# First batch of an attention and mixer kernel: down-sampled sums moved between engines, a smaller mask build, two tiles on other PSUM banks

## The chip, the core and the metric

One core of a Trainium2 chip runs the whole kernel. The metric is the device time of one execution in microseconds. Of the kernel before, three runs took 659.92, 660.85 and 661.27 us; the median is 660.85 us.

## What is computed

The reference, cut to what matters (B = 4 batches, H = 8 heads, S = 576 positions, D = 64 per head, DM = 512):

```python
q_d, k_d, v_d = (t.reshape(B, H, S // 4, 4, D).mean(axis=3) for t in (q, k, v))
low   = repeat(softmax(q_d @ k_d.T / 8) @ v_d, 4, axis=2)
local = softmax(where(abs(i - j) < 4, q @ k.T / 8, -1e9)) @ v
x = (low + local), heads side by side            # B x S x 512
gate = sigmoid(causal 5-tap convolution of x)
x = (gate * (x @ w_val)) @ w_out
h = relu(x.T @ w_tok1) @ w_tok2                  # mixes positions
u = x + h.T
out = u + relu(u @ w_ch1) @ w_ch2
```

## The kernel before

**Stages.** For each batch, `attention(b)` makes x and the gate, `p1(b)` makes u (products with w_val, w_out, w_tok1, w_tok2), and `c1(b)` the first channel product, whose result goes to DRAM. `c2()` does the second channel product for all batches at the end. Large products run three times, as high times high, high times low and low times high parts (`mm3`, lines 217 to 219). The weights arrive as 64-bit words and are decoded on VectorE (lines 135 to 143).

**Order.** Batches 1 to 3 of the attention are mixed into the main stream of products by a table of times, and from `p1(0)` on the order of TensorE is the program's own. Batch 0 comes before all of it, with nothing to hide behind, and its order on each engine is set by a scheduler. `busy(n)` (lines 105 to 108) puts products of zeros between its steps, 80 in all ("fillers", tile `idle_ps`).

**Attention of batch 0.** The four pairs of heads (hp 0 to 3) each go through the same steps:

- `sums` (line 285): q and k of four neighbouring positions are added. In batch 0 this is four matmuls with the identity into PSUM (line 294) and a copy by ScalarE (line 295); in the other batches one `tensor_reduce` of VectorE (line 297). The four parts of v are added in two steps on GpSimd (lines 300 and 301).
- `low_scores` (304) makes the low-resolution scores `sc_d` (line 311), `loc_scores` (347) the local ones `sc_l` in two tiles of 6 and 4 windows: one bf16 matmul writes the mask (line 353), 64x64 matmuls add the scores (line 359).
- `softmax` (251): maximum on VectorE (258), exponentials one window at a time on ScalarE (264), division by the sum on VectorE in batch 0 and on GpSimd in the others (269; the engine is chosen in line 276).
- `low_turn` and `loc_turn` transpose the weights (lines 324, 373), and ScalarE copies them out (327, 377). `low_out` multiplies by the summed v (line 339, tile `o_d`), `loc_out` by v (line 388, tile `o_l`). VectorE adds the two (394), and `conv` follows (401, 404).

After hp 3, `hi_lo` (494 on ScalarE, 495 on GpSimd) splits x, and the first product `p_val` of `p1(0)` can run.

**PSUM.** Eight banks in four tags of two: `as`, `ao`, `m`, `n`. In batch 0, `sc_l` takes both banks of `m`, so the local scores of a pair wait until the exponentials of the pair before have read theirs. `o_d` and `o_l` take `n`, all else but `sc_d` takes `ao`, the fillers too.

**Mask and identity.** GpSimd builds the mask for all ten windows at once (lines 89 to 98); VectorE casts the identity to bf16 (line 88).

**Transfers.** All are issued by SP in a fixed order. A w tile has three buffers, so its load waits for VectorE to have decoded an earlier one.

Of the kernel before, what the change touches and what calls it, by code (L numbers as in the profile page):

```python
# [14 lines left out]
AF = mybir.ActivationFunctionType  # L15
ALU = mybir.AluOpType
AX = mybir.AxisListType
# [3 lines left out]
B, H, S, D = 4, 8, 576, 64  # L21
NHP = H // 2
CQ = 58
WIN = 64
NCK = 10
PADW = CQ * (NCK - 1) + WIN + 3
SD = S // 4
# [30 lines left out]
TAG0 = {"sc_d": "as", "sc_l": "m", "o_d": "n", "o_l": "n"}  # L58
# [12 lines left out]
NEG = -8.0e9  # L71
# [3 lines left out]
def kernel(ctx, tc, qk, vw, v4, w_val, conv_w, w_out, w_tok1, w_tok2, w_ch1, w_ch2, out):  # L75
    nc = tc.nc
# [5 lines left out]
    def T(p, shape, dt, tag, bufs, name=None):  # L82
        return p.tile(shape, dt, tag=tag, bufs=bufs, name=name or tag)

    ident = T(sb, [128, 128], F32, "ident", 1)
    make_identity(nc, ident)
    ident16 = T(sb, [128, 128], BF16, "ident16", 1)
    nc.vector.tensor_copy(out=ident16, in_=ident)
    mask = T(sb, [128, NCK, WIN], BF16, "mask", 1)
    nc.gpsimd.memset(mask, 0.0)  # L90
    for h in range(2):
        m = mask[64 * h:64 * h + 64]
        nc.gpsimd.affine_select(out=m, in_=m, compare_op=ALU.is_ge, fill=NEG, base=0,
                                pattern=[[0, NCK], [1, WIN]], channel_multiplier=-1)
        nc.gpsimd.affine_select(out=m, in_=m, compare_op=ALU.is_ge, fill=NEG, base=6,
                                pattern=[[0, NCK], [-1, WIN]], channel_multiplier=1)
        nc.gpsimd.memset(m[:, 0, 0:3], NEG)
        nc.gpsimd.memset(m[:, NCK - 1, S - (CQ * (NCK - 1) - 3):WIN], NEG)
    cw = T(sb, [128, KC, TAPS], F32, "cw", 1)


# [66 lines left out]
    def w_sq(key, src):  # L168
        return load_w(key, [[r] for r in rows_of(src, 0, DM)], "w2", NW)
# [81 lines left out]
    def softmax(parts, e, scale, mult):  # L251

        P, n, w = e.shape
        mx = T(sb, [P, n], F32, f"mx{P}", NM, name="mx")
        sm = T(sb, [P, n], F32, f"sm{P}", NM, name="sm")
        o = 0
        for p in parts:
            nc.vector.tensor_reduce(out=mx[:, o:o + p.shape[1]], in_=p, axis=AX.X, op=ALU.max)
            o += p.shape[1]
        nc.scalar.activation(out=mx, in_=mx, func=AF.Copy, scale=-scale)  # L260
        o = 0
        for p in parts:
            for c in range(p.shape[1]):
                nc.scalar.activation(out=e[:, o, :], in_=p[:, c, :], func=AF.Exp, scale=scale,  # L264
                                     bias=mx[:, o:o + 1], accum_out=sm[:, o:o + 1])
                o += 1
        nc.scalar.activation(out=sm, in_=sm, func=AF.Copy, bias=1e-9)
        nc.vector.reciprocal(out=sm, in_=sm)
        mult.tensor_tensor(out=e, in0=e, in1=bc(sm, w), op=ALU.mult)

    def attention(b):
# [3 lines left out]
        early = lambda: tc.high_priority(offset=PRI) if b else nullcontext()  # L275
        mult = nc.gpsimd if b else nc.vector

        def bank(shape, name):
            if b:
                tag = "as" if name[:2] == "sc" else "ao"  # L280
            else:
                tag = TAG0.get(name, "ao")
            return T(ps, shape, F32, tag, BANKS[tag], name=name)

        def sums(hp):
            d = hpd[hp]
            w = d.pop("v4")
            qk_d = T(sb, [128, 2, SD], F32, "qkd", ND, name="qk_d")
            qd, kd = qk_d[:, 0], qk_d[:, 1]
            qk_4 = d["qk"][:, :, 3:3 + S].rearrange("p i (a r) -> p i a r", r=4)  # L290
            if b == 0:
                p = bank([128, 2, SD], "qk_d")
                for r in range(4):
                    nc.tensor.matmul(p, lhsT=ident, rhs=qk_4[:, :, :, r], start=(r == 0), stop=(r == 3))  # L294
                nc.scalar.activation(out=qk_d, in_=p, func=AF.Copy)
            else:
                nc.vector.tensor_reduce(out=qk_d, in_=qk_4, axis=AX.X, op=ALU.add)
            d["qkd"] = qd, kd
            vd = T(sb, [72, 2, 128], F32, "vd", NVD, name="vd")
            nc.gpsimd.tensor_tensor(out=w[:, 0:2], in0=w[:, 0:2], in1=w[:, 2:4], op=ALU.add)  # L300
            nc.gpsimd.tensor_tensor(out=vd, in0=w[:, 0], in1=w[:, 1], op=ALU.add)
            d["vd"] = [vd]

        def low_scores(hp):
            d = hpd[hp]
            qd, kd = d.pop("qkd")
            parts = [bank([72, 2, SD], "sc_d") for _ in range(2)]
            for c in range(2):
                for h, p in enumerate(parts):
                    r0 = 64 * h  # L310
                    nc.tensor.matmul(p[:, c, :], lhsT=qd[r0:r0 + 64, c * HD:c * HD + HD],
                                     rhs=kd[r0:r0 + 64, :], start=True, stop=True)
            e = d["ed"] = T(sb, [72, 4, SD], F32, "e", NE, name="e_d")
            softmax(parts, e, 0.125 / 16.0, mult)

        def low_turn(hp):
            d = hpd[hp]
            e = d.pop("ed")
            ts = d["pd"] = []
            for h in range(2):  # L320
                p = bank([72, 2, 2, HD], "pt_d")
                for kc in range(2):
                    for c in range(2):
                        nc.tensor.transpose(p[:, kc, c, :], e[:, 2 * h + c, kc * HD:kc * HD + HD], ident[0:72, 0:72])
                t = T(sb, [72, 2, 2, HD], F32, "pt", NPT, name="pts_d")
                with early():
                    nc.scalar.activation(out=t, in_=p, func=AF.Copy)
                ts.append(t)
# [17 lines left out]
        def loc_scores(hp):  # L346
            d = hpd[hp]
            qk = d["qk"]
            parts = []
            for c0, c1 in LU:  # L350
                n = c1 - c0
                p = bank([128, n, WIN], "sc_l")
                nc.tensor.matmul(p.rearrange("p a w -> p (a w)"), lhsT=ident16,
                                 rhs=mask[:, c0:c1, :].rearrange("p a w -> p (a w)"), start=True, stop=False)
                for c in range(n):
                    o = CQ * (c0 + c)
                    for h in range(2):
                        r0 = 64 * h
                        nc.tensor.matmul(p[r0:r0 + 64, c, :], lhsT=qk[r0:r0 + 64, 0, 3 + o:3 + o + WIN],  # L359
                                         rhs=qk[r0:r0 + 64, 1, o:o + WIN], start=False, stop=(c == n - 1))  # L360
                parts.append(p)
            e = d["el"] = T(sb, [128, NCK, WIN], F32, "e", NE, name="e_l")
            softmax(parts, e, 0.125, mult)
# [50 lines left out]
        if b:  # L414

            hpd[0] = load(b, 0)
            hpd[0]["v"] = load_v(b, 0)
            yield
            sums(0)
            for i in range(NHP + 1):  # L420
                if i < NHP:
                    low_scores(i)
                    yield
                if i:
                    low_turn(i - 1)
                    yield
                if i < NHP:
                    loc_scores(i)
                    yield
                if i + 1 < NHP:  # L430
                    hpd[i + 1] = load(b, i + 1)
                    sums(i + 1)
                if i:
                    low_out(i - 1)
                    yield
                    loc_turn(i - 1)
                    yield
                    loc_out(i - 1)
                    conv(i - 1)
                    yield  # L440
                if i + 1 < NHP:
                    hpd[i + 1]["v"] = load_v(b, i + 1)
# [15 lines left out]
        def scores(hp):  # L458
            loc_scores(hp)
            yield  # L460
            sums(hp)
            low_scores(hp)
            yield
# [258 lines left out]
    w = chain(w_sq("val", w_val), w_sq("out", w_out))  # L722
# [56 lines left out]
```

## Time and profile before

| | |
|---|---|
| median of three runs | 660.85 us (659.92 to 661.27) |
| the profiled execution's own time | 661.05 us |
| its span, first to last instruction | 659.1 us |
| busy: TensorE, its weight loads, VectorE, ScalarE, GpSimd | 622.6, 531.7, 341.6, 300.6, 165.3 us |
| mean granted clock of TensorE | 0.976 of full |
| first `p_val` product / the one from which they run on without a gap | 75.25 us / 81.76 us |

The profiled execution lies 0.2 us over the median, and 1.95 us of its time lie outside the span. In the rows below times count from the start of the span. PE is TensorE, DVE VectorE, ACT ScalarE, POOL GpSimd, and SP issues the transfers. The profile prints some names without their digits: `v_sb` stands for both the tile of four v parts (`v4_sb`, loaded in line 236) and the v windows (loaded in line 245), `ident_68` is the bf16 identity, `w` the 64-bit weight tile. One fp32 matmul call shows as two records.

### The profile page before, as it was taken

How to read it: one execution, taken by the hardware profiler on the slowest of the kernel's cores; microseconds unless marked ns; L12 is line 12 of the kernel's file. 1: busy time of each engine (PE TensorE's matmuls, PEld its weight loads, DVE VectorE, ACT ScalarE, POOL GpSimd, SP SyncE). 2: the span in 40 equal slices, each digit the busy share in tenths (PEclk: the TensorE clock that was granted, in tenths of full speed). 3: DMA queues.
4: the chain of work that ended last, by engine and by line, in shares of the span. 5: the costliest groups of instructions: out<-in, count | busy, mean ns of one | idle time of the engine just before them, and what ended most of it. 6: DMA issues, size and time to landing. Idle time of an engine off the chain costs nothing.

```text
span 659.1 us, 12794 instructions
## 1 busy us (share of the span) xinstructions
PE 622.6 (94%) x4920; PEld 531.7 (81%) x4920; DVE 341.6 (52%) x689; ACT 300.6 (46%) x1032; POOL 165.3 (25%) x183
## 2 busy tenths in 40 slices
PE   6999697988889999999999999999999999999997
PEld 3454496777888988998998999998898888888887
DVE  4478987897886476533344434106637242424232
ACT  1666537555657564547645635324433222222221
POOL 4213521325325413514331413204523000000000
PEclk8999988988889999999999999999999999999999
DMA  8841322456783255783322486565997354553220
GB/s 246 220 150 52 105 61 75 155 184 199 256 287 133 81 192 152 251 250 116 106 71 74 148 252 205 166 191 189 294 311 280 96 161 159 155 164 124 85 79 33
DMA packets 53901, 107.23 MB, mean 163 GB/s; under 512 B 5776, under 2 KB 21392, under 8 KB 53840
## 3 DMA queue, kind: packets, MB, share of 16 engines
q1 hardware_dynamic: 53840, 106.42, 51.5%
q8 instruction: 38, 0.62, 0.4%
q14 instruction: 23, 0.19, 0.1%
HBM read 76.52 MB, written 29.88 MB: 161 GB/s over the span
## 4 chain that ended last, share of the span: by engine, by line
PE 69%; DVE 10%; DMA 8%; ACT 5%; POOL 3%; issue 3%; SPq 0%; DVEq 0%; POOLq 0%; ACTq 0%
PE p_o L217 8%; PE p_o L219 7%; PE p_o L218 7%; PE g_ps L217 5%; DMA w<-in_w_ch_dram 5%; PE g_ps L218 5%; PE g_ps L219 4%; PE sc_l L359 3%; DMA v_sb<-in_v_dram 2%; PE p_val L218 2%; PE qk_d L294 2%; PE p_val L217 2%; PE p_val L219 2%; ACT e_l L264 2%; PE p_x L217 2%
## 5 line engine op out<-in xcount | busy, mean ns | idle before, releaser
L217 PE MATMUL g_ps<-u_hl,w_hl 128*128 128x288 f32 x384 | 117.0, 305 | 0.7 <-DVE u_sb L612 0.7
L218 PE MATMUL g_ps<-u_hl,w_hl 128*128 128x288 f32 x384 | 114.1, 297 | 1.2 <-POOL u_hl L495 1.1
L219 PE MATMUL g_ps<-u_hl,w_hl 128*128 128x288 f32 x384 | 113.5, 296 | 0.0
L217 PE MATMUL p_o<-g_hl,ch 128*128 128x512 f32 (+1 forms) x240 | 88.7, 370 | 0.9 <-ACT r_sb L641 0.9
L219 PE MATMUL p_o<-g_hl,ch 128*128 128x512 f32 (+1 forms) x240 | 88.5, 369 | 0.0
L218 PE MATMUL p_o<-g_hl,ch 128*128 128x512 f32 (+1 forms) x240 | 88.5, 369 | 0.0
L495 DVE TENSOR_TENSOR g_hl<-r_back,g_hl 128x512 fp32r<-128x512 f32 (+1 forms) x60 | 38.4, 641 | 92.9 <-ACT g_hl L494 87.4
L494 ACT ACTIVATE g_hl<-r_back 128x512 fp32r<-128x512 f32 (+1 forms) x60 | 35.2, 588 | 107.5 <-PE p_o L219 105.2
L217 PEld LDWEIGHTS g_ps<-u_hl,w_hl 128*128 128x128 f32 x384 | 72.4, 189 | 4.0 <-issue 2.7
L218 PEld LDWEIGHTS g_ps<-u_hl,w_hl 128*128 128x128 f32 x384 | 72.6, 189 | 2.1 <-POOL u_hl L495 2.1
L219 PEld LDWEIGHTS g_ps<-u_hl,w_hl 128*128 128x128 f32 x384 | 72.6, 189 | 0.0
L641 ACT ACTIVATE r_sb<-g_ps 128x288 f32<-128x288 f32 x96 | 39.0, 408 | 57.8 <-PE g_ps L219 50.3
L404 DVE SCALAR_TENSOR_TENSOR gate_sb<-x_f,cw,gate_sb 128x575 f32<-128x575 f32 (+5 forms) x68 | 60.7, 900 | 0.8
L217 PEld LDWEIGHTS p_o<-g_hl,ch 128*128 128x128 f32 x240 | 45.2, 188 | 9.3 <-ACT r_sb L641 1.7
L219 PEld LDWEIGHTS p_o<-g_hl,ch 128*128 128x128 f32 x240 | 45.2, 189 | 7.7
L218 PEld LDWEIGHTS p_o<-g_hl,ch 128*128 128x128 f32 x240 | 45.3, 189 | 7.6
L264 ACT ACTIVATE e_l<-sc_l,mx 128x64 f32<-128x64 f32 x160 | 48.2, 332 | 0.8
L495 POOL TENSOR_TENSOR x_hl<-x_f,x_hl 128x288 fp32r<-128x288 f32 x32 | 32.5, 1028 | 59.9 <-ACT x_hl L494 59.9
L217 PE MATMUL p_val<-x_hl,val_hi 128*128 128x288 f32 x128 | 41.1, 321 | 5.2 <-ACT x_hl L494 3.1
L218 PE MATMUL p_val<-x_hl,val_hi 128*128 128x288 f32 x128 | 40.0, 313 | 1.5 <-POOL x_hl L495 1.5
L135 DVE TENSOR_SCALAR wa<-w 128x256 int32<-128x256 int32 (+2 forms) x76 | 25.1, 343 | 30.8 <-DMA w<-in_w_ch_dram 16.9
L217 PE MATMUL p_x<-y_hl,out_hi 128*128 128x288 f32 x128 | 39.8, 311 | 1.4 <-ACT u_sb L546 0.7
(110 smaller groups left out, 1324.2 us busy)
## 6 DMA issues: line engine op xcount, KB each, us to landing
w_hl<-w_dr SPq DMA_DIRECT2D x36, 512.0 KB, 4.4
r_dr<-r_sb SPq DMA_DIRECT2D x48, 288.0 KB, 4.3
w<-in_w_ch_dram SPq DMA_DIRECT2D x48, 256.0 KB, 3.2
r_back<-r_dr SPq DMA_DIRECT2D x48, 256.0 KB, 2.8
qk_sb<-in_qk_dram SPq DMA_DIRECT2D x16, 589.0 KB, 4.0
w_dr<-w_hl SPq DMA_DIRECT2D x12, 512.0 KB, 2.9
v_sb<-in_vw_dram SPq DMA_DIRECT2D x16, 320.0 KB, 13.7
v_sb<-in_v_dram SPq DMA_DIRECT2D x16, 288.0 KB
```

The costliest lines, as they stand in the source:

```text
L135: nc.vector.tensor_scalar(a, high, 3, 0x3FFFFFF8, ALU.logical_shift_left, ALU.bitwise_and)
L217: nc.tensor.matmul(out_ap, lhsT=lh, rhs=rh, start=first, stop=False)
L218: nc.tensor.matmul(out_ap, lhsT=lh, rhs=rl, start=False, stop=False)
L219: nc.tensor.matmul(out_ap, lhsT=ll, rhs=rh, start=False, stop=last)
L264: nc.scalar.activation(out=e[:, o, :], in_=p[:, c, :], func=AF.Exp, scale=scale, bias=mx[:, o:o + 1], accum_out=sm[:, o:o + 1])
L294: nc.tensor.matmul(p, lhsT=ident, rhs=qk_4[:, :, :, r], start=(r == 0), stop=(r == 3))
L359: nc.tensor.matmul(p[r0:r0 + 64, c, :], lhsT=qk[r0:r0 + 64, 0, 3 + o:3 + o + WIN], rhs=qk[r0:r0 + 64, 1, o:o + WIN], start=False, stop=(c ...
L404: nc.vector.scalar_tensor_tensor(out=g[:, t0:s1], in0=x[:, t0 - sh:s1 - sh], scalar=cw[:, hp, k:k + 1], in1=g[:, t0:s1], op0=ALU.mult, op1 ...
L494: nc.scalar.activation(out=hi_ap, in_=src_ap, func=AF.Copy)
L495: lo_eng.tensor_tensor(out=lo_ap, in0=src_ap, in1=hi_ap.bitcast(F32), op=ALU.subtract)
L641: paced[0] = nc.scalar.activation(out=r[:, hv(hs)], in_=p[:, 0:HS], func=AF.Relu)
```

## The change

The bf16 identity is built by GpSimd. The mask's pattern is built for one window and copied to the others, all on GpSimd. In batch 0 the sums of q and k are made by VectorE's `tensor_reduce`, as in the other batches; the four identity matmuls and ScalarE's copy go. The v parts of batch 0 are not added beforehand: `low_out` runs over all four, so `o_d` accumulates 16 matmul calls for a pair of heads and not 4. The local scores of hp 1 take the banks `n`. The line that chooses the engine of the softmax division is the same in both kernels.

```diff
@@ -85,17 +85,20 @@
     ident = T(sb, [128, 128], F32, "ident", 1)
     make_identity(nc, ident)
     ident16 = T(sb, [128, 128], BF16, "ident16", 1)
-    nc.vector.tensor_copy(out=ident16, in_=ident)
+    make_identity(nc, ident16)
     mask = T(sb, [128, NCK, WIN], BF16, "mask", 1)
-    nc.gpsimd.memset(mask, 0.0)
+    one = mask[:, 1, :]
+    nc.gpsimd.memset(one, 0.0)
     for h in range(2):
-        m = mask[64 * h:64 * h + 64]
+        m = one[64 * h:64 * h + 64]
         nc.gpsimd.affine_select(out=m, in_=m, compare_op=ALU.is_ge, fill=NEG, base=0,
-                                pattern=[[0, NCK], [1, WIN]], channel_multiplier=-1)
+                                pattern=[[1, WIN]], channel_multiplier=-1)
         nc.gpsimd.affine_select(out=m, in_=m, compare_op=ALU.is_ge, fill=NEG, base=6,
-                                pattern=[[0, NCK], [-1, WIN]], channel_multiplier=1)
-        nc.gpsimd.memset(m[:, 0, 0:3], NEG)
-        nc.gpsimd.memset(m[:, NCK - 1, S - (CQ * (NCK - 1) - 3):WIN], NEG)
+                                pattern=[[-1, WIN]], channel_multiplier=1)
+    nc.gpsimd.tensor_copy(out=mask[:, 0, :], in_=one)
+    nc.gpsimd.tensor_copy(out=mask[:, 2:, :], in_=one.unsqueeze(1).to_broadcast([128, NCK - 2, WIN]))
+    nc.gpsimd.memset(mask[:, 0, 0:3], NEG)
+    nc.gpsimd.memset(mask[:, NCK - 1, S - (CQ * (NCK - 1) - 3):WIN], NEG)
     cw = T(sb, [128, KC, TAPS], F32, "cw", 1)
 
 
@@ -275,11 +278,11 @@
         early = lambda: tc.high_priority(offset=PRI) if b else nullcontext()
         mult = nc.gpsimd if b else nc.vector
 
-        def bank(shape, name):
+        def bank(shape, name, tag=None):
             if b:
                 tag = "as" if name[:2] == "sc" else "ao"
             else:
-                tag = TAG0.get(name, "ao")
+                tag = tag or TAG0.get(name, "ao")
             return T(ps, shape, F32, tag, BANKS[tag], name=name)
 
         def sums(hp):
@@ -288,14 +291,11 @@
             qk_d = T(sb, [128, 2, SD], F32, "qkd", ND, name="qk_d")
             qd, kd = qk_d[:, 0], qk_d[:, 1]
             qk_4 = d["qk"][:, :, 3:3 + S].rearrange("p i (a r) -> p i a r", r=4)
+            nc.vector.tensor_reduce(out=qk_d, in_=qk_4, axis=AX.X, op=ALU.add)
+            d["qkd"] = qd, kd
             if b == 0:
-                p = bank([128, 2, SD], "qk_d")
-                for r in range(4):
-                    nc.tensor.matmul(p, lhsT=ident, rhs=qk_4[:, :, :, r], start=(r == 0), stop=(r == 3))
-                nc.scalar.activation(out=qk_d, in_=p, func=AF.Copy)
-            else:
-                nc.vector.tensor_reduce(out=qk_d, in_=qk_4, axis=AX.X, op=ALU.add)
-            d["qkd"] = qd, kd
+                d["vd"] = [w[:, r] for r in range(4)]
+                return
             vd = T(sb, [72, 2, 128], F32, "vd", NVD, name="vd")
             nc.gpsimd.tensor_tensor(out=w[:, 0:2], in0=w[:, 0:2], in1=w[:, 2:4], op=ALU.add)
             nc.gpsimd.tensor_tensor(out=vd, in0=w[:, 0], in1=w[:, 1], op=ALU.add)
@@ -349,7 +349,7 @@
             parts = []
             for c0, c1 in LU:
                 n = c1 - c0
-                p = bank([128, n, WIN], "sc_l")
+                p = bank([128, n, WIN], "sc_l", "n" if hp == 1 else None)
                 nc.tensor.matmul(p.rearrange("p a w -> p (a w)"), lhsT=ident16,
                                  rhs=mask[:, c0:c1, :].rearrange("p a w -> p (a w)"), start=True, stop=False)
                 for c in range(n):
```

The lines of the kernel after are shifted by three. Three places show how the order of instructions moves.

GpSimd, from the mask to its first work on data, before (`v_sb` is the tile of four v parts):

```order
L93 AFFINE_SELECT mask<-mask 64x640 x2
L95 AFFINE_SELECT mask<-mask 64x640 x2
L97 MEMSET mask 64x3
L98 MEMSET mask 64x7
L300 TENSOR_TENSOR v_sb<-v_sb 72x512
L97 MEMSET mask 64x3
L98 MEMSET mask 64x7
L301 TENSOR_TENSOR vd<-v_sb 72x256
```

and of the change:

```order
L96 AFFINE_SELECT mask<-mask 64x64 x2
L98 COPY mask<-mask 128x64
L99 COPY mask<-mask 128x512
L100 MEMSET mask 128x3
L101 MEMSET mask 128x7
L495 TENSOR_TENSOR x_hl<-x_f_113,x_hl 128x288
L300 TENSOR_TENSOR v_sb<-v_sb 72x512
L301 TENSOR_TENSOR vd<-v_sb 72x256
L300 TENSOR_TENSOR v_sb<-v_sb 72x512
L301 TENSOR_TENSOR vd<-v_sb 72x256
L300 TENSOR_TENSOR v_sb<-v_sb 72x512
L495 TENSOR_TENSOR x_hl<-x_f_114,x_hl 128x288
```

The second pair of memsets no longer stands behind the sum of v. The sums that follow are those of batch 1; three of them now stand between the split of x of hp 0 (`x_f_113`) and that of hp 1.

TensorE at the scores of hp 1, before:

```order
L294 MATMUL qk_d<-qk_sb,ident 128x288
L353 LDWEIGHTS ident_68
L353 MATMUL sc_l<-mask,ident_68 128x384
L359 MATMUL sc_l<-qk_sb 64x64 x12
L294 MATMUL qk_d<-qk_sb,ident 128x288
L353 LDWEIGHTS ident_68
L353 MATMUL sc_l<-mask,ident_68 128x256
L359 MATMUL sc_l<-qk_sb 64x64 x8
L294 MATMUL qk_d<-qk_sb,ident 128x288 x2
```

and of the change, from the scores of hp 2 on (20 fillers, `sc_d` of hp 0 and `sc_l` of hp 0 and hp 1 stand ahead of it; `pt_d_339` and `pt_d_346` are the transposes of hp 0):

```order
L353 LDWEIGHTS ident16_68
L353 MATMUL sc_l_394<-mask_73,ident16_68 128x384
L359 MATMUL sc_l_394<-qk_sb_171 64x64 x12
L353 LDWEIGHTS ident16_68
L353 MATMUL sc_l_408<-mask_73,ident16_68 128x256
L359 MATMUL sc_l_408<-qk_sb_171 64x64 x8
L311 MATMUL sc_d_314<-qk_d_312 72x144 x2
L311 MATMUL sc_d_315<-qk_d_312 72x144 x2
L324 MATMUL pt_d_339<-ident_63,e_d_244 72x72 x4
L324 MATMUL pt_d_346<-ident_63,e_d_244 72x72 x4
L111 LDWEIGHTS idle_92
L111 MATMUL idle_ps_353<-idle_92 128x512
```

The local scores of three pairs now stand one behind the other, with no filler between them; 59 of the 80 fillers come behind these rows.

ScalarE at the end of batch 0, from the copy of `o_d` of hp 3 to the split of its x, before:

```order
L343 ACTIVATE x_f_113<-o_d 128x576
L344 ACTIVATE x_f_113<-o_d 128x4
L412 ACT_TABLE_LOAD
L412 ACTIVATE gate_sb<-gate_sb 128x288 x3
L401 ACTIVATE gate_sb<-x_f_113,cw 128x288 x2
L142 ACTIVATE out_hi<-wa 128x256 x2
L412 ACTIVATE gate_sb<-gate_sb 128x288 x3
L494 ACTIVATE x_hl<-x_f_113 128x288
```

and of the change:

```order
L343 ACTIVATE x_f_116<-o_d 128x576
L344 ACTIVATE x_f_116<-o_d 128x4
L412 ACTIVATE gate_sb<-gate_sb 128x288
L145 ACTIVATE out_hi<-wa 128x256
L412 ACTIVATE gate_sb<-gate_sb 128x288 x2
L145 ACTIVATE out_hi<-wa 128x256
L412 ACTIVATE gate_sb<-gate_sb 128x288
L401 ACTIVATE gate_sb<-x_f_116,cw 128x288 x2
L494 ACTIVATE x_hl<-x_f_116 128x288
```

The five other steps that stood between the gate's first tap (L401) and the split (L494) now stand ahead of the first tap. From the first `p_val` on, the order of TensorE is the same in both kernels.

## Rows read from the trace of the kernel before

**Rows 1.** The page, part 2: 40 slices of 16.5 us, TensorE's granted clock in tenths.
```profile
PEclk8999988988889999999999999999999999999999
```

**Rows 2.** Busy by stretch: PE, PEld, DVE, ACT, POOL (instructions), PEclk, DMA share, GB/s.
```profile
0.00:81.76 81.76, 70.52 (x566) 35.74 (x566) 55.37 (x127) 44.85 (x189) 28.75 (x32) 0.95 0.54 156
81.76:659.00 577.24, 552.12 (x4354) 495.99 (x4354) 286.25 (x563) 255.70 (x843) 136.53 (x151) 0.98 0.52 164
```

**Rows 3.** Chain of waits, 0 to 80 us: start, duration, what.
```profile
2.61 8.97 DMA v_sb<-in_v_dram
...
22.06 0.85 PE sc_l L359 x24
...
31.13 0.32 PE idle_ps L108
...
33.26 0.70 PE pt_l L373 x5
...
34.35 1.48 PE idle_ps L108 x6
...
43.66 0.65 PE sc_d L311 x8
44.31 0.72 PE o_l L388 x20
...
45.79 0.53 PE pt_d L324 x8
...
53.41 4.15 PE qk_d L294 x8
```

**Rows 4.** Timeline, TensorE: start, duration, instruction, idle before it and releaser.
```profile
13.33 0.48 PE L353 MATMUL sc_l<-mask,ident 128*128 128x384 bf16 x1 [4.47 <-POOL mask L98]
...
33.88 0.47 PE L339 MATMUL o_d<-pts_d,vd 72*64 72x144 f32 x4
...
164.65 0.71 PE L339 MATMUL o_d<-pts_d,vd 72*64 72x144 f32 x8
```

**Rows 5.** Line 297 (VectorE's sums, other batches): ns min/median/max.
```profile
L297 DVE TENSOR_REDUCE qk_d<-qk_sb x12: 1333/1350/1357, 90.4 to 326.6; 128x288 f32<-128x1152 f32 x12
```

**Rows 6.** Timeline and chain: steps of VectorE and ScalarE in the softmax of batch 0.
```profile
12.95 0.29 DVE L135 TENSOR_SCALAR wa<-w 128x256 int32<-128x256 int32 x1 [3.50 <-DMA w<-in_w_val_dram]
...
16.82 0.42 DVE L258 TENSOR_REDUCE mx<-sc_l 128x4 f32<-128x256 f32 x1
...
18.31 0.20 ACT L260 ACTIVATE mx<-mx 128x10 f32<-128x10 f32 x1
...
27.47 2.96 ACT e_l L264 x20
...
113.79 0.36 ACT e_d L264 x2
```

**Rows 7.** Busy by stretch, as rows 2: where TensorE's clock is low.
```profile
13.00:19.00 6.00, 5.61 (x48) 3.19 (x47) 4.16 (x13) 1.80 (x7) 1.61 (x4) 0.50 1.04 274
82.00:87.00 5.00, 5.00 (x22) 5.00 (x23) 3.51 (x11) 2.07 (x5) 0.00 (x0) 0.50 0.00 0
```

**Rows 8.** Timeline, the end of batch 0 on four engines.
```profile
73.39 0.81 PE L388 MATMUL o_l<-pts_l,v_sb 64*64 64x58 f32 x38
76.09 0.81 DVE L394 TENSOR_TENSOR x_f<-o_l,x_f 128x290 f32<-128x290 f32 x2
76.94 0.96 ACT L401 ACTIVATE gate_sb<-x_f,cw 128x288 f32<-128x288 f32 x2 [1.41 <-DVE x_f L394]
79.42 1.33 POOL L300 TENSOR_TENSOR v_sb<-v_sb 72x512 f32<-72x512 f32 x1 [3.40 <-DMA v_sb<-in_v_dram]
79.42 0.43 ACT L494 ACTIVATE x_hl<-x_f 128x288 fp32r<-128x288 f32 x1
80.71 1.00 POOL L495 TENSOR_TENSOR x_hl<-x_f,x_hl 128x288 fp32r<-128x288 f32 x1
```

**Rows 9.** Timeline, GpSimd: the split of x of hp 1.
```profile
61.76 6.08 POOL L495 TENSOR_TENSOR x_hl<-x_f,x_hl 128x288 fp32r<-128x288 f32 x1 [7.63 <-ACT x_hl L494]
```

## The prediction

> **What bounds the kernel now.** I read the busy time by stretch first. From 81.76 us on, TensorE is busy 552 of 577 us in an order that the change leaves alone [rows 2], so whatever batch 0 gains or loses there reaches the end nearly whole, and the forecast is the shift of one moment: 81.76, from which the products of `p_val` run on. Ahead of it TensorE works 70.5 of 81.8 us, VectorE 55, ScalarE 45, GpSimd 29 [rows 2].
>
> Second, the chain of waits up to there. It begins with a transfer: the first tile of v parts lands at 11.58, GpSimd adds it, and only then writes the last two pieces of the mask; TensorE, which had stood still for 4.47 us, starts the first scores at 13.33 [rows 3, 4]. From there the chain lies mostly on TensorE's own work: the four sums of q and k (4.15 us where one runs undisturbed), fillers, scores, transposes [rows 3]. ScalarE's exponentials hold it up once, 2.96 us for the ten of a pair [rows 6].
>
> Third, the end. The last `o_l` is done at 74.20, but `p_val` runs on only at 81.76, 7.6 us later [rows 8]: the addition, ScalarE's first tap (which waited 1.41 us for it), five other steps of ScalarE, the copy, a sum of v on GpSimd that had waited for its transfer until 79.42, and the split of x.
>
> Fourth, the clock. The page shows it a little under full at the start [rows 1]. By stretch it is at 0.50, the lower level of 1.2 GHz, from 13 to 19 us, right behind the wait of 4.47 us, and again from 82 to 87, behind the gaps of the tail [rows 7].
>
> **Part by part.**
>
> Mask and identity. The order of GpSimd shows that all but the last two pieces of the old mask were written before the sum of v. The new one is smaller, apart from a copy of 512 columns; the trace has no such copy, so I bound it between nothing and GpSimd's addition of 512 columns, 1.33 us [rows 8]. Either way it ends well before 11.58, without a transfer ahead of it. Price zero; the cover is the same stretch in which TensorE waited. The cast on VectorE that goes is too small and early to count.
>
> Where the start is then bound. The wait of 4.47 us goes, but not all of it is gained: on VectorE the second maximum of hp 0 now stands behind the first step on the third weight piece, which starts at 12.95, when its transfer lands, and takes 0.29; with the maximum, 0.42, that is 13.66 [rows 6]. From here ScalarE sets the pace, because scores of hp 1 have their own banks and no longer wait for it: scaling 0.20 (13.9), ten exponentials 2.96 with two weight copies at about 0.43 between them (17.7), four low exponentials at 0.36 and three small steps (19.7), the ten of hp 1 (22.7), a small step, and the copy of the first `pts_d`, again about 0.43, at 23.3 [rows 6, 8]. There the first `o_d` product can run. TensorE has done 20 fillers and the scores of three pairs by then, and waits for most of the time from 14 to 23.
>
> TensorE after 23.3, in its new order. 58 fillers: six in a row take 1.48, one alone shows 0.32 [rows 3]; I take 0.32, thus 18.6, because in the new order they stand in short groups between steps that wait for VectorE and ScalarE, and the 4.1 us over the lower price are my allowance for those waits. `o_d`: 16 calls for a pair and not 4, 64 in all, 128 records. The only rows for it are 0.47 for four records and 0.71 for eight [rows 4], which give 0.118 and 0.089 for one; the run of 16 calls is nearest to the longer row, so 128 x 0.089 = 11.4 (15.0 by the other). `o_l`: 8 x 0.72 = 5.8. Transposes of the local weights: 4 x 0.70 = 2.8. `sc_d` of two pairs: 2 x 0.65 = 1.3. Transposes of the low weights, three pairs: 3 x 0.53 = 1.6 [rows 3]. Local scores of hp 3: 40 records at 0.85 for 24, and two mask products, of which 0.48 is the slow price, 1.9 together [rows 3, 4]. Sum 43.4. Four fillers come behind the last `o_l`, beside the tail: 1.3 off. So the last `o_l` ends at 23.3 + 42.1 = 65.4 at full clock.
>
> The four sums that go from TensorE, 16.6 us at 4.15, are inside this comparison, and their four copies on ScalarE with them. What `o_d` grows by pays back about half of it: 48 more calls, 96 records, 8.5 us.
>
> VectorE's sums. The same instruction runs twelve times in the other batches, 1.35 us each [rows 5]. Four are 5.4 us more on an engine that had 26 us idle ahead of 81.76 [rows 2]. Two stand ahead of 13.7, where VectorE waits for transfers; the two others run in the shadow of the exponentials. I cost them at zero; if the idle time does not cover them they cost up to 5.4 (below). The Trainium skill speaks against this move: "VectorE: DVE Perf Modes", section "Rules for kernel authors", calls `tensor_reduce` on the hot path the slowest operation of that engine and advises restructuring. The twelve rows only show its price, not whether it is on the path; by that rule the sum would lose all four.
>
> GpSimd loses eight additions of v. In their place the splits of x of hp 1 to 3 stand behind three sums of batch 1. Each waits for a load that follows the one before: 3.40 us for one [rows 8], say 5.5 with its sums, so some 17 us after the `o_d` of hp 0, before 60. No cost. SP issues the same transfers, with v of batch 1 moved forward among the w pieces.
>
> Clock. TensorE waits more before 23.3 than it did before 13.33, where 6 us at 0.50 followed [rows 4, 7]. I assume the same 6 us again: 3.0 lost, giving 68.4.
>
> Tail. By its instructions alone it is 0.81 + 0.96 + 0.43 + 1.00 = 3.2; before it was 7.6 [rows 8]. Five steps of ScalarE, 77.90 to 79.42, now run ahead of the first tap (1.5 us), and GpSimd's sum of v, until 80.75, is not in front of the split (1.3). VectorE's lateness with the addition, about 1.9 after 74.20, I keep. So 7.6 - 1.5 - 1.3 = 4.8, and `p_val` runs on at 73.2.
>
> Softmax products on VectorE: batch 0 had them there already; no cost and no gain.
>
> **Sum.** 73.2 against 81.76 is -8.6 us. The profiled execution took 661.05, of which 1.95 lie outside the span: 661.05 - 8.6 = 652.45. It lies 0.2 over the median of the runs, so I say 652.3.
>
> **Rivals.**
>
> *The clock holds.* The scores of three pairs and fillers may be spread enough that the clock does not fall, and the tail comes to its 3.2. Then 3.0 or, with the tail, 4.6 us more are gained: 647.7 to 649.3. Against it: after both long stretches of waiting it was at 0.50 [rows 7].
>
> *The clock stays low: slower than before.* If the gaps in the new order keep TensorE at 1.2 GHz from 23.3 on, each us of that stretch does half the work. 3 us are already in the sum; the gain of 8.6 is used up when 11.6 are lost, that is when the clock is low until 23.3 + 23.2 = 46.5. Low until 55 it loses 15.9, or 12.9 over my sum: +4.3, 665.1. For it: the sums of q and k, which filled TensorE between the steps, are gone. Against it: 58 fillers are placed for this, and before, 6 us were enough [rows 7]. The Trainium skill, "TensorE: Matmul & The Clock Gate", section "HAM oscillation — how this bites in real kernels", says that waits between groups of matmuls can set the clock back each time; rows 7 show that happen once after a wait, and no row here shows it repeating.
>
> *VectorE becomes the bound.* Besides the sums it has the weight decoding, the softmax and the gate. If all four sums lie on the path, 5.4 of the 8.6 go: 657.7. For it: 55 of 82 us were busy already and the stretch gets shorter [rows 2].
>
> *GpSimd's split is slow again.* That of hp 1 took 6.08 us instead of 1.00 beside VectorE's work [rows 9, 8]. On the last one this costs 5.1: 657.4. Against it: the last one took 1.00 beside a similar run of VectorE.
>
> **How the numbers follow.** My forecast has 0.55 (its own range 649.5 to 656), the held clock 0.13, VectorE 0.13, the slow split 0.10, the low clock 0.09. Between the bounds of the unknown costs lie 3.6 us for `o_d`, 4.1 for the fillers downwards, -1.6 and +2.8 for the tail. The range 647.5 to 660.0 takes in all but the low clock and a tenth of the rest. A measurement of this kernel can tell about 0.2%, 1.3 us, from no change: faster 0.83, same 0.07 (the two losing rivals together with a dearer `o_d`), slower 0.10 (the low clock, or losses of three rivals added).
>
> **What would show it.** Right: no sum of q and k on TensorE; first exponentials at about 14 and the first `o_d` at 23 to 24; a clock of 0.50 for some 6 us around there and not later; `o_d` at 0.09 a record; the last `o_l` near 68 and `p_val` running on near 73; the stretch behind it as long as before. Wrong: `o_d` at 0.12 or more; TensorE waiting for VectorE's sums or maxima all through; GpSimd's last split late; a clock at half beyond 46; or the main stream giving the gain back because weights of `w_tok` arrive no earlier.

## The result

| | before | the changed kernel |
|---|---|---|
| median, us | 660.91 (659.37 to 661.96, 8 runs) | 654.34 (650.64 to 656.90, 8 runs) |
| the profiled execution: time, span | 661.05, 659.1 | 653.42, 651.6 |
| first scores of batch 0 / first `o_d` of hp 0 | 13.33 / 32.80 | 9.03 / 21.65 |
| `p_val` runs on from | 81.76 | 78.69 |
| first `p_x` | 89.5 | 83.9 |

The ratio is 0.9895 [0.9864, 0.9927]: 6.6 us faster by the medians, 7.6 by the two profiled executions. The forecast was 8.6, to 652.3. The runs of the changed kernel differ by 6 us among themselves, and nearly in the order of their mean granted clock: 0.971 with 650.64, 0.966 with 653.42, 0.959 with 656.90.

TensorE's granted clock on the page of the changed kernel, which answers to [rows 1]:

```profile
PEclk9695898988979999999999999999999999999999
```

The low tenths stand in the second and fourth slice now. The busy time by stretch (columns as in [rows 2]), which answers to [rows 2, 7], shows them closer:

```profile
0.00:14.00 14.00, 11.98 (x112) 6.02 (x113) 9.16 (x23) 4.13 (x15) 3.05 (x17) 1.00 0.89 278
14.00:23.00 9.00, 5.88 (x63) 3.30 (x62) 7.99 (x18) 9.00 (x57) 0.00 (x0) 0.87 1.01 274
23.00:30.00 7.00, 7.00 (x20) 2.83 (x20) 2.98 (x8) 3.70 (x23) 0.00 (x0) 0.50 0.41 149
...
40.00:50.00 10.00, 8.54 (x105) 5.41 (x103) 10.00 (x17) 4.92 (x29) 4.87 (x4) 1.00 0.41 139
50.00:60.00 10.00, 8.11 (x47) 4.26 (x49) 9.66 (x20) 4.49 (x17) 2.09 (x2) 0.57 0.32 107
60.00:70.00 10.00, 9.95 (x79) 6.51 (x78) 3.47 (x10) 2.94 (x7) 0.22 (x1) 0.58 0.09 28
...
80.00:90.00 10.00, 8.95 (x66) 8.49 (x65) 9.98 (x22) 4.74 (x13) 3.74 (x4) 1.00 0.06 20
```

TensorE's clock is at half twice, from 23 to 30 and, which I had not forecast, over most of 50 to 70; from 40 to 60 VectorE is busy 19.7 of 20 us. Behind 80, where the kernel before ran at 0.50 [rows 7], the clock is full.

What stood in front of the second low stretch is in the timeline of the changed kernel (start, duration, instruction, idle before it and its releaser):

```profile
45.81 0.79 PE L388 MATMUL o_l<-pts_l,v_sb 64*64 64x58 f32 x20
46.53 1.47 PE L111 MATMUL idle_ps<-idle 128*128 128x512 bf16 x6
47.85 0.69 PE L324 MATMUL pt_d<-ident,e_d 72*72 72x72 f32 x8
51.89 1.33 PE L388 MATMUL o_l<-pts_l,v_sb 64*64 64x58 f32 x20 [3.35 <-DVE x_f L394]
```

TensorE stands still for 3.35 us, and from here the 20 records of `o_l` take 1.33 and not 0.79. Behind VectorE's addition (L394) the same view shows who was late:

```profile
44.61 0.41 DVE L261 TENSOR_REDUCE mx<-sc_l 128x4 f32<-128x256 f32 x1
...
48.20 0.46 ACT L145 ACTIVATE out_hi<-wa 128x256 fp32r<-128x256 f32 x1
...
48.33 1.34 DVE L294 TENSOR_REDUCE qk_d<-qk_sb 128x288 f32<-128x1152 f32 x1
...
49.01 0.66 ACT L343 ACTIVATE x_f<-o_d 128x576 f32<-128x576 f32 x1
...
50.96 0.20 ACT L344 ACTIVATE x_f<-o_d 128x4 f32<-128x4 f32 x1
...
51.39 0.45 DVE L394 TENSOR_TENSOR x_f<-o_l,x_f 128x290 f32<-128x290 f32 x1
```

The second maximum of hp 3 ends at 45.0, behind the taps of the gate of hp 0 on VectorE. ScalarE's exponentials of hp 3 follow it and fill ScalarE to 48.2; only behind them comes its copy of `o_d` of hp 1 at 49.01, whose small rest (L344) ends at 51.16. VectorE's addition needs this copy, and TensorE needs the bank that the addition frees. VectorE itself is no earlier: a sum of batch 1 (48.33), weight decoding and a softmax division of hp 3 keep it busy until the addition at 51.39.

### The profile page after: what moved, and what is told of

It reads as the page before. It is cut to its first block, busy times and chain, and to the rows that moved or that the text cites. A ratio compares the mean times of both kernels' runs of the same rounds, so it can differ in the third digit from the quotient of the medians.

```text
span 651.6 us, 12905 instructions
## 1 busy us (share of the span) xinstructions
PE 618.0 (95%) x4984; PEld 533.1 (82%) x4984; DVE 344.5 (53%) x692; ACT 297.7 (46%) x1028; POOL 150.4 (23%) x177
## 4 chain that ended last, share of the span: by engine, by line
PE 69%; DVE 12%; DMA 8%; ACT 7%; POOL 2%; issue 2%; SPq 1%; DVEq 0%; ACTq 0%; POOLq 0%
PE p_o L220 7%; PE p_o L222 7%; PE p_o L221 7%; PE g_ps L220 5%; PE g_ps L221 5%; PE g_ps L222 5%; DMA w<-in_w_ch_dram 5%; ACT e_l L267 3%; PE sc_l L359 2%; PE o_d L339 2%; PE p_val L220 2%; PE p_val L221 2%; PE p_val L222 2%; DVE gate_sb L404 2%; PE p_x L220 2%
## 5 line engine op out<-in xcount | busy, mean ns | idle before, releaser
L494 ACT ACTIVATE g_hl<-r_back 128x512 fp32r<-128x512 f32 (+1 forms) x60 | 35.2, 588 | 107.5 <-PE p_o L222 105.1
L641 ACT ACTIVATE r_sb<-g_ps 128x288 f32<-128x288 f32 x96 | 38.9, 406 | 55.9 <-PE g_ps L222 48.2
L495 POOL TENSOR_TENSOR x_hl<-x_f,x_hl 128x288 fp32r<-128x288 f32 x32 | 27.4, 868 | 103.6 <-ACT x_hl L494 61.9
L220 PE MATMUL p_val<-x_hl,val_hi 128*128 128x288 f32 x128 | 40.3, 315 | 4.2 <-DVE y L533 4.2
L221 PE MATMUL p_val<-x_hl,val_hi 128*128 128x288 f32 x128 | 38.8, 303 | 0.9 <-POOL x_hl L495 0.7
L222 PE MATMUL p_val<-x_hl,val_lo 128*128 128x288 f32 x128 | 38.5, 300 | 0.0
```

The lines of the kernel that those rows point to most:

```text
L220: nc.tensor.matmul(out_ap, lhsT=lh, rhs=rh, start=first, stop=False)
L221: nc.tensor.matmul(out_ap, lhsT=lh, rhs=rl, start=False, stop=False)
L222: nc.tensor.matmul(out_ap, lhsT=ll, rhs=rh, start=False, stop=last)
L494: nc.scalar.activation(out=hi_ap, in_=src_ap, func=AF.Copy)
L495: lo_eng.tensor_tensor(out=lo_ap, in0=src_ap, in1=hi_ap.bitcast(F32), op=ALU.subtract)
L641: paced[0] = nc.scalar.activation(out=r[:, hv(hs)], in_=p[:, 0:HS], func=AF.Relu)
```

## The experiments

The theories: **A**, TensorE's own work bounds batch 0, as my sum had it; **B**, VectorE (with ScalarE) bounds it, and TensorE's products are hidden; **C**, each engine is late in turn, so that parts of the change overlap. All medians stand beside those of the kernel before in the same measurement, 660.7 to 661.2 us.

**The q and k sums back on TensorE** (`u_qk`).

```diff
+            if b:
                 nc.vector.tensor_reduce(out=qk_d, in_=qk_4, axis=AX.X, op=ALU.add)
+            else:
+                p = bank([128, 2, SD], "qk_d")
+                for r in range(4):
+                    nc.tensor.matmul(p, lhsT=ident, rhs=qk_4[:, :, :, r], start=(r == 0), stop=(r == 3))
+                nc.scalar.activation(out=qk_d, in_=p, func=AF.Copy)
```

> The changed kernel with the q and k sums of batch 0 back as identity matmuls and a ScalarE copy; all else as changed. Theory A (TensorE's own work bounds batch 0 and the sums of 4.15 us for a pair were its largest removable piece): slower than the changed kernel's 654.3 by 4 to 9 us, 658 to 663, with few waits of TensorE left. Theory B (in the changed kernel VectorE and ScalarE bound batch 0, TensorE waits and the clock falls): the sums fill waits that are there anyway and keep the clock up, so 0 to 3 us slower, or even up to 2 faster, 652 to 657, and the stretch of half clock from 52 to 68 us goes.

Measured: 653.25 us (650.72 to 653.59), 0.988 [0.9839, 0.9921]. Nothing is lost, so A falls for this part. The gain of 1.1 us by the medians is not clear of the noise. The stretch to 78 us in this kernel:

```profile
0.00:78.00 78.00, 74.39 (x672) 41.57 (x673) 59.89 (x137) 46.00 (x192) 13.50 (x26) 1.00 0.57 169
```

TensorE is busy for 74 of 78 us at full clock. The sums cost it nothing net, because without them it waits and then runs at half.

**The v sums back on GpSimd** (`u_v`).

```diff
-            if b == 0:
-                d["vd"] = [w[:, r] for r in range(4)]
-                return
```

> The changed kernel with the v parts of batch 0 added on GpSimd again, so that o_d has 4 calls for a pair and not 16. Theory A: 48 calls less on TensorE at 0.14 to 0.18 us are 7 to 8.5 us less work on the bounding engine, so 4 to 8 us faster than the changed kernel, 646 to 650: the v part of the change was a loss. Theory B: TensorE waits for VectorE and ScalarE instead, so within 2 us of the changed kernel, 652 to 656, with longer waits of TensorE.

Measured: 654.40 (650.09 to 657.44), 0.9895 [0.9847, 0.9944]. Its longest waits on TensorE (who waited for whom: us in total, times, longest):

```profile
PE idle_ps L111 <- ACT pts_d L324: 4.1, 3, 3.6
PE p_val L220 <- ACT x_hl L491: 2.6, 1, 2.6
PE pt_d L321 <- DVE e_d L272: 2.1, 1, 2.1
PE sc_l L350 <- POOL mask L101: 1.9, 1, 1.9
```

The 96 records fewer come back as waits for ScalarE and VectorE, as B said for the whole time. Batch 0 alone looks less clear: in the profiled execution the first `p_x` comes at 80.89, 3.0 us before that of the changed kernel, though the span ends 0.8 us later. The last row is new: in this order the last memset of the mask stands behind a v sum again, and 1.9 us of the wait return.

**The scores of hp 1 back on the banks m** (`u_bank`).

```diff
-                p = bank([128, n, WIN], "sc_l", "n" if hp == 1 else None)
+                p = bank([128, n, WIN], "sc_l", None)
```

> The changed kernel with the local scores of hp 1 back on the banks m. Theory A: the scores of hp 1 wait for the exponentials of hp 0 and the fillers and products behind them come later; ScalarE loses its back-to-back exponentials: 2 to 5 us slower than the changed kernel, 656 to 659. Theory B (the exponentials of hp 3, VectorE's gate work and the banks n around 48 us are what bounds, far behind these scores): within 1.5 us, 653 to 656.

Measured: 653.80 (649.63 to 655.22), 0.9883 [0.9832, 0.9934]; no difference from the changed kernel. The wait that A expected is there, and paid for elsewhere:

```profile
PE sc_l L353 <- ACT e_l L267: 5.3, 1, 5.3
PE o_l L388 <- ACT x_f L344: 1.4, 1, 1.4
```

TensorE waits 5.3 us early and only 1.4 where it waited 3.35. In this profiled execution the first `p_x` comes at 79.99, 3.9 us earlier than in the changed kernel, and the rest takes as much longer; so "no difference" holds for the end, and not for batch 0.

**The new mask and identity alone, in the kernel before** (`o_mask`).

```diff
-    nc.vector.tensor_copy(out=ident16, in_=ident)
+    make_identity(nc, ident16)
...
-    nc.gpsimd.memset(mask, 0.0)
+    one = mask[:, 1, :]
+    nc.gpsimd.memset(one, 0.0)
...
```

> The kernel before with only the new mask and identity build. Theory A (the wait of 4.47 us at 13.33 was on the path): up to 4.5 us faster than 660.9, likely 2 to 4, 657 to 659, as the first scores start at about 9 and all moves up. Theory B (behind it comes the next late thing: transfers of q and k and the second maximum behind the weight decoding): within 1 us, 660 to 662.

Measured: 657.78 (652.08 to 661.26, 12 runs), 0.9955 [0.9924, 0.9986]: 3.4 us by the medians, as A had it. The profiled execution, 652.08, is the fastest of the twelve. In it the first scores begin at 8.62, and the order leaves a rest of the wait:

```profile
8.62 0.34 PE L356 MATMUL sc_l<-mask,ident 128*128 128x384 bf16 x1
...
11.35 0.27 PE L356 MATMUL sc_l<-mask,ident 128*128 128x256 bf16 x1 [1.54 <-POOL mask L101]
```

**The v part alone, in the kernel before** (`o_v`).

```diff
+            if b == 0:
+                d["vd"] = [w[:, r] for r in range(4)]
+                return
             vd = T(sb, [72, 2, 128], F32, "vd", NVD, name="vd")
```

> The kernel before with the v part of the change alone: batch 0 has no v sums on GpSimd, o_d has 16 calls for a pair. The order of GpSimd then has the whole mask ahead of any v sum, so the wait of 4.47 us at 13.33 goes here too. Theory A (TensorE's own work bounds batch 0): 8.5 us more products against 4.5 of wait, so 2 to 5 us slower than the kernel before's 661. Theory B (VectorE and ScalarE bound most of batch 0, the start excepted): the added products lie in waits, and 2 to 4 us are gained as with the new mask alone, 657 to 659.

Measured: 657.67 (654.62 to 659.51), 0.9947 [0.9925, 0.9969]. As B had it: 3.6 us gained with 96 records more on TensorE. Without the v sum nothing stands ahead of the old mask either, so this part and the mask part remove the same wait. The next late thing shows in its timeline:

```profile
9.02 0.34 PE L356 MATMUL sc_l<-mask,ident 128*128 128x384 bf16 x1 [2.06 <-DVE ident L88]
```

It is the cast of the identity, 0.22 us long, behind the first weight decoding on VectorE. I had called it too small and too early to count; its place counted, not its length.

**The q and k part alone, in the kernel before** (`o_qk`).

```diff
-            if b == 0:
-                p = bank([128, 2, SD], "qk_d")
...
-            else:
-                nc.vector.tensor_reduce(out=qk_d, in_=qk_4, axis=AX.X, op=ALU.add)
+            nc.vector.tensor_reduce(out=qk_d, in_=qk_4, axis=AX.X, op=ALU.add)
```

> The kernel before with the q and k part alone: the sums on VectorE, the mask wait still there. Theory A: 16.6 us less on TensorE, 5 to 9 us faster than 661, 652 to 656, nearly the whole gain of the change. Theory B: the wait at 13.33 stays, VectorE gets 5.4 us more; 0 to 2 us faster, 659 to 661, and the granted clock falls in more of batch 0.

Measured: 655.45 (651.03 to 659.93, 12 runs), 0.9904 [0.9875, 0.9934]. A's number, although the wait for the mask is still there. Its runs spread over 9 us, from a mean clock of 0.972 with 651.03 to 0.952 with 659.93. Of the slowest, the stretch to 81 us and two waits:

```profile
0.00:81.00 81.00, 65.53 (x538) 37.08 (x539) 63.54 (x131) 43.00 (x185) 26.08 (x32) 0.74 0.54 157
```
```profile
PE sc_l L347 <- POOL mask L98: 4.6, 1, 4.6
PE idle_ps L108 <- ACT pts_d L321: 3.6, 1, 3.6
```

So the parts alone give 3.4, 3.6 and 5.8 us, 12.8 together, and all of them 6.6 (the banks were not run alone). That is C: they overlap. Some 3.5 of the difference is the wait that two parts share; where the rest overlaps is not shown.

**The softmax divisions on GpSimd** (`x_mult`), from the changed kernel. `mult` is `nc.gpsimd` in batch 0 too.

```diff
-        mult = nc.gpsimd if b else nc.vector
+        mult = nc.gpsimd
```

> The changed kernel with the softmax divisions of batch 0 on GpSimd, as in the other batches: eight operations, about 6.3 us at 0.75 to 0.82, go from VectorE to GpSimd. Theory B (VectorE bounds from about 38 us to the first p_val): 2 to 5 us faster than the changed kernel, 649 to 652. Theory A: the division is on the way to the transposes and takes longer on GpSimd, so 0 to 3 us slower, 654 to 657. If VectorE is late only at one place (48 us), within 1.5 us.

Measured: 651.88 (649.46 to 656.37), 0.9875 [0.9844, 0.9907]: 2.5 us faster by the medians, which B would allow, but its interval reaches over that of the changed kernel. Not shown.

**No fillers between the steps** (`nw1_0`), from the changed kernel.

```diff
-NW0, NW1 = 8, 3
+NW0, NW1 = 8, 0
```

> The changed kernel without the 72 fillers between the steps of batch 0 (the 8 ahead of it stay). Theory A without a clock effect: about 50 fillers at 0.25 us less on the bounding engine, so 8 to 12 us faster, 642 to 646. Theory B with the clock: TensorE's work is hidden anyway, the clock falls to half for most of batch 0 and into the products of p_val, so 0 to 8 us slower than the changed kernel, 654 to 662, with a granted clock of 0.5 over 20 us or more before 90.

Measured: 651.13 (650.39 to 652.96, 4 runs), 0.9857 [0.9832, 0.9882]. Neither theory: by the medians 3.2 us faster (its interval and that of the changed kernel overlap), with the clock at half nearly throughout.

```profile
0.00:16.00 16.00, 10.78 (x125) 6.39 (x126) 10.69 (x28) 5.85 (x26) 3.05 (x17) 1.00 0.91 275
16.00:71.00 55.00, 48.26 (x435) 39.49 (x433) 42.42 (x96) 36.21 (x159) 10.06 (x9) 0.50 0.47 142
71.00:80.00 9.00, 8.73 (x54) 8.41 (x55) 9.00 (x23) 4.58 (x13) 1.78 (x3) 0.81 0.24 60
```

TensorE's real products, at half clock for 55 us, still end early enough. In the changed kernel the fillers keep the clock up for about half of that stretch, and this is worth no more than what they cost: there six take 1.47 us at full clock, and two take 1.03 at half.

**Each VectorE sum made twice** (`v_double`), from the changed kernel.

```diff
-            nc.vector.tensor_reduce(out=qk_d, in_=qk_4, axis=AX.X, op=ALU.add)
+            for _ in range(1 if b else 2):
+                nc.vector.tensor_reduce(out=qk_d, in_=qk_4, axis=AX.X, op=ALU.add)
```

> The changed kernel with each q and k sum of batch 0 made twice on VectorE, so 4 x 1.35 = 5.4 us more there and nothing else changed. Theory B (VectorE and ScalarE bound batch 0): 3 to 6 us slower than the changed kernel, 657 to 660. Theory A (TensorE bounds): within 1.5 us, 653 to 656. Theory C (no engine alone: each is late in turn, and one's extra work lies partly in another's wait): 1 to 3 us slower.

Measured: 659.32 (653.68 to 662.53, 12 runs), 0.9981 [0.9951, 1.0012]: 5.0 us slower than the changed kernel, for 5.4 us of work added; the two intervals lie apart. By the whole time that is B. The chain of waits of this kernel to 24 us:

```profile
4.54 1.35 DVE qk_d L295
...
6.10 1.26 DVE qk_d L295
...
9.63 1.26 DVE qk_d L295
...
13.52 0.34 DVE mx L261
13.88 0.22 ACT mx L263
14.12 0.70 ACT e_l L267 x4
...
23.84 0.67 PE o_d L340 x2
```

From 4.54 to 13.88 the chain lies on VectorE. The first exponentials start at 14.12, in the changed kernel at 12.36; the first `o_d` comes at 23.84 and not at 21.7. Not all of the loss lies in batch 0, though: the first `p_x` comes at 85.71, 1.9 us later than in the changed kernel, and the other 3.6 of the 5.5 us between the two profiled executions come behind it. The share of batch 0 is what C had, and what the second set costs behind it is not shown.

**No fillers, in the kernel before** (`o_nw1_0`): the edit of `nw1_0` there.

> The kernel before without its 72 fillers between the steps. The changed kernel lost 3 us by this at a clock of half nearly all through. If the fillers are on TensorE's path in the kernel before as well (it had more work there and few waits): 6 to 12 us faster than 661, 649 to 655, so that most of what the change brings is had by leaving them out. If the clock they hold is worth what they cost in this kernel: within 3 us of 661.

Measured: 654.09 (649.53 to 655.88), 0.9897 [0.9861, 0.9933]. Leaving the fillers out of the kernel before brings 6.6 us, as much as the whole change, although the clock up to 81.76 us is then 0.75 and not 0.95 [rows 2].

**Two versions to beat both.** `best_a` is the changed kernel with the edits of `nw1_0` and `x_mult`; `best_b` is that of `u_qk` with the edit of `x_mult`, fillers kept.

> The changed kernel without fillers between the steps and with the softmax divisions of batch 0 on GpSimd. Theory B (with the fillers gone, VectorE is what is late): 2 to 4 us faster than without fillers alone, 647 to 649. Theory D (at half clock TensorE's own products fill the stretch from 23 to 72 us, so it bounds again): the same as without fillers alone, 650 to 652.

> The changed kernel with the q and k sums back on TensorE, the fillers kept, and the softmax divisions of batch 0 on GpSimd: VectorE has 5.4 + 6.3 us less than in the changed kernel and TensorE 16.6 more. Theory B (VectorE bounds): 3 to 6 us faster than the changed kernel's 654, 648 to 651. Theory A (TensorE bounds): slower than with the sums back alone (653.3), 654 to 658. Theory C (each engine late in turn): 651 to 653, with the clock full through batch 0.

Measured: `best_a` 649.86 (647.14 to 653.01), 0.9856 [0.9816, 0.9897], the fastest median of all, 10.9 under the kernel before and 4.5 under the changed one, though the intervals of these two overlap; over `nw1_0` 1.3, which settles nothing. `best_b` 654.51 (650.98 to 655.06), 0.9913 [0.9878, 0.9947]: B fails here. With the sums on TensorE, relieving VectorE gains nothing; its TensorE waits for little more than

```profile
PE idle_ps L111 <- ACT pts_d L332: 1.7, 2, 1.4
PE sc_l L358 <- ACT e_d L267: 1.0, 1, 1.0
```

(the second wait lies in batch 1, behind 82 us) and the clock stays mostly full. There TensorE is the bound. Both ends of C are seen: which engine is late depends on what the version put on it.

## Why the prediction came out as it did

The measured time lies in the range and in that of the likeliest case; the sum of 8.6 was 2.0 too large, and it came that near only because wrong terms cancelled. By its steps:

- **The start** was right in kind. The wait for the mask goes (13.33 to 9.03), and the two experiments that remove it alone gain 3.4 and 3.6. I had the decoding step ahead of the second maximum and the ScalarE pace; the first `o_d` came at 21.65 and not 23.3, because the third weight piece was there at 11.45 and not 12.95.
- **VectorE's sums at zero** held, but with no room to spare. The chain of waits of the changed kernel still begins with a transfer (start, duration, what):

```profile
3.49 7.94 DMA w<-in_w_val_dram
11.45 0.29 DVE wa L138
11.75 0.34 DVE mx L261
```

  VectorE comes to this step straight from its second sum, as its timeline shows:

```profile
4.65 1.35 DVE L294 TENSOR_REDUCE qk_d<-qk_sb 128x288 f32<-128x1152 f32 x1 [3.72 <-DMA qk_sb<-in_qk_dram]
...
8.89 1.35 DVE L294 TENSOR_REDUCE qk_d<-qk_sb 128x288 f32<-128x1152 f32 x1
...
10.83 0.55 DVE L261 TENSOR_REDUCE mx<-sc_l 128x6 f32<-128x384 f32 x1
```

  The second sum, two weight steps and the first maximum end at 11.38, only 0.07 us before the weight step that waited for its piece. The other two sums of batch 0 (14.93 and 20.43) run while the chain lies on ScalarE's exponentials. So the single sums are not on the chain; a second set is, at the start. The Trainium skill, "VectorE: DVE Perf Modes", section "Rules for kernel authors", calls this reduction the slowest operation of VectorE and advises to consider restructuring it on a hot path; here the four sums, 1.35 us each, stayed just beside the path.
- **The bound behind the first `o_d`** is the step that failed. My sum has TensorE's own work there, with 4.1 us for waits. In the chain of waits the stretch from 28.3 to 51.9 lies on VectorE: maxima, weight decoding, taps of the gate and a sum of batch 1, with one transfer of a weight piece between them (31.5 to 37.9). The rival "VectorE becomes the bound" named the right engine, but for the sums of batch 0, which are not in that stretch.
- **The four sums off TensorE** (16.6 us) are worth 5.8 in the kernel before and nothing clear of the noise, 1.1 the other way, in the changed one. They were not removable time but partly cover for waits.
- **`o_d`** I had at 0.089 us a record; 32 records take 2.18 at full clock, 0.068. **Fillers** run at 0.245 in a row of six (1.47), where I took 0.32. Together some 7 us too much, of which the 4.1 for the fillers were meant as an allowance for waits.
- **The waits and the clock** took it: one wait of 3.35 us at 48.5, which no term named, and two low stretches instead of one. From 51.9 to 68 us the clock is at half, 16 us, some 8 lost, and from 21 to 31, some 5 lost, where the sum had 3 in all. The Trainium skill, "TensorE: Matmul & The Clock Gate", section "HAM oscillation — how this bites in real kernels", says that waits between groups of products can set the clock back each time; this trace now shows it repeating, each time right behind a stop (1.40 us at 21.14, 3.35 at 51.89), though not behind every one: after 1.63 us at 14.59 the clock stayed full.
- **The tail** took 3.1 us, 75.57 to 78.69, its own instructions' 3.2 and not my 4.8: VectorE was not late with the addition.
- **The balance.** `p_val` ran on 5.5 us later than the 73.2 of the sum. The low clock (10 more than allowed) and the long wait (3.4) are too little in it, the start (1.7), the prices (7) and the tail (1.7) too much; the other 2.5 are smaller pieces. Behind it the shift grew from 3.1 to 7.5 us. That the end came within 2.0 of the forecast is luck.
- **"Passes nearly whole"** was wrong in a useful way. At 78.69 only 3.1 us of the gain were there. From `p_val` to the first `p_x` it took 7.7 us before and 5.2 now, since the clock is full there; with the rest of the way the shift grew to 7.5 at the end. The products behind 81.76 are less of a block than "552 of 577 us" says. From 90 to 200 us, before and now, TensorE stands still for some 15 of 110 us:

```profile
90.00:200.00 110.00, 95.39 (x893) 83.94 (x892) 92.11 (x206) 63.94 (x239) 36.97 (x35) 0.92 0.56 182
90.00:200.00 110.00, 95.12 (x926) 83.54 (x926) 87.24 (x201) 66.90 (x260) 38.22 (x37) 0.92 0.58 187
```

  From the first `p_x` to the end it took 569.6 us before, 567.8 in the changed kernel and 566.9 to 571.9 over all fourteen profiled executions, though no experiment edits anything behind batch 0. So a difference of up to 5 us between two profiled executions need not come from batch 0. Why this stretch varies was not traced.
- **The rival of a low clock** had the wrong price. In the changed kernel the clock was at half for 26 us in all, some 13 lost, more than the 11.6 at which I had the gain used up; still 6.6 were gained, because the sum was too dear elsewhere. `nw1_0`, without fillers, ran at half from 16 to 71 and took 651.13; my +4.3 assumed that the fillers stay on the path.

What stays open: why runs of one kernel get low stretches of different length. That the spread follows the clock is seen in the clocks of the runs alone, since one execution of each kernel was profiled.

## What to carry to other kernels

An engine with a third of a stretch idle can still be the one that the first steps wait for: price an added instruction by what stands behind it in its queue there, not by the busy share of the whole stretch. Before adding up what several parts of a change bring, ask whether two of them remove the same wait (here the mask and the v part did, 3.4 and 3.6 alone). Try leaving fillers out again after each change: here they cost more than the clock they held was worth, 6.6 us in the kernel before and, by the medians, 3.2 in the changed one. Mark a moment behind the changed stretch, here the first `p_x`, and compare it as well as the end: what comes behind it varied here by up to 5 us, against a gain of 6.6.

## What was not expected of the hardware

The two versions with the lowest mean granted clock, `best_a` (0.935 to 0.949) and `nw1_0` (0.940 to 0.946), have the two fastest medians, 649.86 and 651.13 us; `u_qk`, at 0.984 to 0.989, took 653.25. Between kernels the mean clock does not order the times; between runs of one kernel it nearly ordered them, 0.972 to 0.952 with 651.03 to 659.93 in `o_qk`.
